# A gated-linear-attention and soft-mixture kernel, rewritten from pairs of heads over whole sequences to units of 128 tokens with all heads

## The chip, the cores and the metric

The kernel runs on one NeuronCore of a Trainium2 chip. The metric is device time in microseconds (us) of one execution. PE is TensorE (matmuls; PEld are its weight loads), DVE is VectorE, ACT is ScalarE, POOL is GpSimd, and SP is the queue that issues all DMA transfers. All data is float32. In the profile a float32 matmul stands as two MATMUL instructions, and a transpose as one.

## The reference

```python
# B, H, S, D = 4, 8, 768, 48; N = B * S = 3072 tokens of 384 columns; 8 experts of 4 slots, F = 1024
f = 1 / (1 + exp(-f_logit))
for t in range(S):                                    # per batch b and head h, state is D x D
    state = f[t][:, None] * state + outer(k[t], v[t])
    y[t] = q[t] @ state
x = y.transpose(0, 2, 1, 3).reshape(3072, 384)
logits = x @ phi                                      # 3072 x 32 slots
d = softmax(logits, over the tokens); c = softmax(logits, over the slots)
slot_input = d.T @ x                                  # 32 x 384
slot_out[e] = relu(slot_input[e] @ w1[e]) @ w2[e]     # 8 experts, 4 slots each
out = c @ slot_out                                    # 3072 x 384
```

## The kernel before

**Attention, one pair of heads at a time.** 32 heads (4 sequences x 8) are 16 pairs; a pair lies on 112 partitions, 64 r + d for head r and channel d, with all 768 tokens along the free axis. f, k and q of a pair come as six loads of 48 rows (`load_dqk`, L226 to L230), v as two of 64 rows (L232 to L235). DVE makes the decays of all 768 tokens: it adds 1 to exp(-f) (L252), and runs a scan (`decay_scan`, L258) that multiplies them up and starts anew every 64 tokens, which gives G; ACT takes its logarithm and the inverse (L266, L270), POOL multiplies k by G (L262) and q by P = 1 / G (L282). PE transposes k' (L290), makes 64x64 blocks of scores k' against q' (L302), which DVE masks (L305), and the products k'^T v of all 12 chunks (L321). A second scan on DVE (`state`, L334), with P at the chunks' ends spread over the columns (L275), carries the state through all chunks at once. The outputs are masked scores times v (`intra`, L348) and q' times states (`inter`, L362, whose moving operand takes every ninth or fourth column of the scan's result); ACT copies them to x (L367).

**Mixture.** As soon as a sequence is done, its x is transposed (L383), multiplied by phi (L390), exponentiated under a running maximum, and summed into the slots' inputs (L450). After the last pair the last sequence does the same in pieces (L399 to L418), then come the experts: `up` (L592), transposes of the hidden values (`turn`, L602), `down` in column parts of 232 and 152 (L629), the sum of the slots' columns (L643), and `combine` (L654), which multiplies the softmax over the slots by slot_out, in two parts of 12 bits at one pass per matmul. Copies (L657) and stores (L661) follow.

**Order.** The program is a list of (time, function) sorted by time (`at`, `run_atoms`); the times are a period T = 7.6 a pair and offsets in OFF, moved by tables (FK, CK, TK). They set only the order: `keep_order` makes each engine take its instructions as written. SP's queue is one of these engines. w1 is loaded during the attention, w2 into buffers as the attention leaves them.

## Time and profile before

| what | value |
|---|---|
| runs | 227.75, 230.16, 230.81 us; median 230.16 us |
| profiled execution | span 228.6 us, first to last instruction; the median of the runs lies 1.6 us above |
| busy share of the span | PE 86%, PEld 65%, DVE 78%, ACT 42%, POOL 29% |
| DMA | 49.35 MB, mean 216 GB/s; 28536 packets, 18512 of them under 2 KB |
| granted TensorE clock | 0.892 of full, mean over the span |

The span is the time from the first to the last instruction of one profiled execution. A row of a timeline gives start, duration, engine, source line, operation, output and input and count; a row of a group gives count, busy time and the mean of one in ns, then the engine's idle time before it and what ended that. A row of a window gives each engine's busy time (and count of instructions) in that stretch, then the granted clock, the DMA engines' busy share and the rate.

### The profile page before, as it was taken

How to read it: one execution, taken by the hardware profiler on the slowest of the kernel's cores; microseconds unless marked ns; L12 is line 12 of the kernel's file. 1: busy time of each engine (PE TensorE's matmuls, PEld its weight loads, DVE VectorE, ACT ScalarE, POOL GpSimd, SP SyncE). 2: the span in 40 equal slices, each digit the busy share in tenths (PEclk: the TensorE clock that was granted, in tenths of full speed). 3: DMA queues.
4: the chain of work that ended last, by engine and by line, in shares of the span. 5: the costliest groups of instructions: out<-in, count | busy, mean ns of one | idle time of the engine just before them, and what ended most of it. 6: DMA issues, size and time to landing. Idle time of an engine off the chain costs nothing.

```text
span 228.6 us, 6760 instructions
## 1 busy us (share of the span) xinstructions
PE 197.4 (86%) x2782; PEld 149.2 (65%) x2782; DVE 178.4 (78%) x322; ACT 96.9 (42%) x208; POOL 66.0 (29%) x62
## 2 busy tenths in 40 slices
PE   6598799889799599999959979999999899989820
PEld 6577678677678386887838567887756435547710
DVE  6999999999999899999998999999892352204640
ACT  7444346435575224567525255562323323103420
...
GB/s 169 230 131 200 201 229 178 244 241 252 246 220 185 95 135 149 258 211 231 206 202 108 278 181 159 233 0 217 335 289 342 346 204 326 378 179 125 339 316 66
DMA packets 28536, 49.35 MB, mean 216 GB/s; under 512 B 3664, under 2 KB 18512, under 8 KB 28496
## 3 DMA queue, kind: packets, MB, share of 16 engines
q1 hardware_dynamic: 28496, 48.82, 74.7%
...
HBM read 44.09 MB, written 4.72 MB: 214 GB/s over the span
## 4 chain that ended last, share of the span: by engine, by line
DVE 55%; PE 29%; DMA 7%; issue 4%; ACT 2%; DVEq 0%; ACTq 0%
DVE sb L334 18%; DVE gb L258 10%; DVE pb L275 7%; DMA w1b<-in_w_dram 7%; DVE scb L305 5%; PE py L362 4%; DVE eb L252 4%; DVE kvp L331 3%; PE py L348 3%; PE pi L450 3%; PE kvp L321 3%; PE pf L654 3%; PE ph L592 2%; PE po L629 2%; PE psc L302 2%
## 5 line engine op out<-in xcount | busy, mean ns | idle before, releaser
L334 DVE TENSOR_TENSOR_SCAN sb<-kvp,pb 48x432 f32<-48x432 f32 (+1 forms) x64 | 51.1, 798 | 1.3
L262 POOL TENSOR_TENSOR kb<-kb,gb 112x768 f32<-112x768 f32 (+1 forms) x17 | 29.7, 1749 | 64.0 <-DVE gb L258 51.2
L362 PE MATMUL py<-sb,qb 112*64 112x96 f32 x352 | 39.8, 356 | 0.0
L302 PE MATMUL psc<-qb,kb 48*64 48x64 f32 x768 | 32.3, 240 | 3.9 <-POOL vb L200 2.6
L302 PEld LDWEIGHTS psc<-qb,kb 48*64 48x64 f32 x768 | 26.3, 147 | 12.5 <-issue 6.1
L282 POOL TENSOR_TENSOR qb<-qb,eb 112x768 f32<-112x768 f32 (+1 forms) x15 | 26.7, 1778 | 23.4 <-ACT eb L270 22.6
L362 PEld LDWEIGHTS py<-sb,qb 112*64 112x64 f32 x352 | 27.5, 159 | 5.4 <-issue 2.5
L258 DVE TENSOR_TENSOR_SCAN gb<-eb,d 112x768 f32<-112x768 f32 (+1 forms) x17 | 28.3, 1664 | 1.6
L348 PE MATMUL py<-vb,scb 128*64 128x96 f32 x384 | 29.2, 272 | 0.0
L321 PE MATMUL kvp<-vb,ktb 128*48 128x96 f32 (+1 forms) x384 | 22.6, 272 | 5.5 <-DVE sb L334 3.9
L348 PEld LDWEIGHTS py<-vb,scb 128*64 128x64 f32 x384 | 24.4, 153 | 4.2 <-issue 3.2
L321 PEld LDWEIGHTS kvp<-vb,ktb 128*48 128x48 f32 x384 | 20.1, 143 | 7.8 <-DVE sb L334 5.3
L367 ACT COPY xb<-py 128x384 f32<-128x384 f32 (+1 forms) x32 | 12.7, 398 | 23.5 <-PE py L362 23.5
L248 ACT ACTIVATE eb<-fb 112x768 f32<-112x768 f32 (+1 forms) x17 | 13.6, 803 | 19.2 <-POOL qb L282 12.4
L275 DVE COPY pb<-eb 112x384 f32<-112x384 f32 (+1 forms) x32 | 20.7, 690 | 0.5
L266 ACT ACTIVATE eb<-gb 112x768 f32<-112x768 f32 (+1 forms) x17 | 13.7, 809 | 10.4 <-DVE gb L258 10.4
L290 PE MATMUL pk<-ident,kb 112*128 112x112 f32 x96 | 17.8, 304 | 0.0
L291 ACT COPY ktb<-pk 128x336 f32<-128x336 f32 x32 | 13.8, 437 | 7.4 <-PE pk L290 7.3
L305 DVE TENSOR_TENSOR scb<-psc,mask 128x384 f32<-128x384 f32 x32 | 16.4, 551 | 0.3
L270 ACT ACTIVATE eb<-eb 112x768 f32<-112x768 f32 (+1 forms) x17 | 13.7, 808 | 0.3
L290 PEld LDWEIGHTS pk<-ident,kb 112*128 112x128 f32 x96 | 10.9, 157 | 3.2 <-issue 0.7
L252 DVE TENSOR_SCALAR eb<-eb 112x768 f32<-112x768 f32 (+1 forms) x17 | 10.3, 606 | 1.2 <-ACT eb L248 1.2
(181 smaller groups left out, 277.6 us busy)
## 6 DMA issues: line engine op xcount, KB each, us to landing
...
```

The lines of the kernel that those rows point to most:

```text
L252: nc.vector.tensor_scalar(e, e, 1.0, G_LIM, op0=ALU.add, op1=ALU.min)
L258: nc.vector.tensor_tensor_scan(part(own(gb, i), h), e, d, 1.0, op0=ALU.mult, op1=ALU.min)
L262: (nc.gpsimd if ENG["dk"] == 2 or i < 2 else nc.vector).tensor_tensor(t, t, part(use(gb, i), h), op=ALU.mult)
L275: eng("pend")(t[:PW, :, : c1 - c0], e[:, c0:c1].unsqueeze(1).broadcast_to([PW, D, c1 - c0]))
L282: (nc.gpsimd if i > 1 and ENG["dq"] == 2 or (i, h) == (1, 1) else nc.vector).tensor_tensor(t, t, part(use(eb[i % NEB], i), h), op=ALU.mult)
L290: nc.tensor.transpose(pk[:, mm], kq[:PW, 128 * m : 128 * m + 128], ident[:PW, :PW])
L302: nc.tensor.matmul(scp[i, r][64 * j : 64 * j + 64, 64 * m : 64 * m + 64], kq[rs, cs], qq[rs, cs], start=True, stop=True)
L305: nc.vector.tensor_tensor(own(scb[i % NSC], i)[:, r], scp[i, r][:, : NM * C].rearrange("q (m t) -> q m t", t=C), mask.unsqueeze(1).broadca ...
L321: nc.tensor.matmul(pk[64 * r : 64 * r + D, cs], kr[:, m, 64 * r : 64 * r + D], vv[:, :nj, m, r], start=True, stop=True)
L334: nc.vector.tensor_tensor_scan(st[h][rs, r].rearrange("p e c -> p (e c)"), kvh[rs, : D * n], pe[rs].rearrange("p e c -> p (e c)"), 0.0, op ...
L348: nc.tensor.matmul(py[64 * w : 64 * w + 64, M - Ms[0], :, r], sc[:, r, m], vv[:, :, m, r], start=M == Ms[0] and r == 0, stop=False, skip_g ...
L362: nc.tensor.matmul(py[64 * w : 64 * w + 64, M - Ms[0], j], qt[:PW, C * c : C * c + C], sc, start=False, stop=(M, j) == (Ms[-1], 1), skip_g ...
```

## The change

The whole program is another. It has 12 units of 128 tokens instead of 16 pairs of 768 tokens: unit u holds tokens 128 (u // 2) to 128 (u // 2) + 127 of the two sequences 2 (u % 2) and 2 (u % 2) + 1, with all 8 heads of both: 16 heads, as 8 pairs `a` on partitions 64 r + d. The gate sums are made by PE: softplus(-f) of a unit (one exp and one ln on ACT, tokens on partitions) is multiplied by a triangle of ones (`d_cum`, 8 matmuls of 128x128x128), and ACT makes G and P from the result (`d_g`, `d_p`). Chunks are still 64 tokens (j = 0, 1), with the decay running over both; the state is carried by three adds and products of 384 columns on DVE (`state_1`, `state_t`, `state_2`) in place of the scans. `kv`, `inter`, `scores` and `intra` are 32 matmuls each of one head and one chunk (`inter` in two halves of 16, one before `scores`, one after `intra`), placed so that consecutive ones lie in the four quarters of the array (rows 0 or 64, columns 0 or 64) and the two row halves write different PSUM banks. PSUM is four tiles of two banks: PA for gate sums and the mixture, PB for outputs, PC for the transposes of k', then kv, then the transposes of x, PD for scores. Every load has 128 rows: k and q come padded to 64 channels, 4 KB a row, w1 and w2 as 16 pieces each of 128 rows of 6 KB. The mixture works on groups of two units (256 tokens of two sequences). w2 and the output are split in two column halves, one load a piece; `combine` is a float32 product of 32 rows for each of four 32-row groups. The warm-up matmuls that stood at the start are no longer called. The order is again a sorted list, with T = 6.9.

```diff
...
-NCH = S // C  # chunks of a sequence
-NM = NCH // 2  # pairs of chunks
-NG = NM // 2  # blocks of 256 tokens
+L = 128
+NU = 12
+NV = 6
...
+T = 6.9
+OFF = dict(
+    lf=6.2 - 4 * T, lk=4.4 - 3 * T, lq=6.6 - 3 * T, lv=6.5 - 2 * T,
+    exp=4.25 - 2 * T, ln=5.3 - 2 * T, cum=0.9 - T, g=1.95 - T, p=3.1 - T, dk=3.1 - T, dq=5.55 - T, pend=8.0 - T,
+    kt=0, ktok=0.95, kv=2.1, s1=2.8, p2=3.5, sc=3.75, st=3.4, mask=4.5, intra=5.9, p1=6.2,
+    y=T + 0.1, s2=T + 1.1, xt=T + 4.45, xe=T + 5.75,
+    lg=2 * T + 5.2, mx=2 * T + 5.7, et=2 * T + 6.3, tr=3 * T + 5.2, el=3 * T + 5.7, pin=4 * T + 5.2, join=4 * T + 5.7,
+)
...
+    PA, PB, PC, PD = (pp.tile([128, 2, 512], F32, tag=n, name=n) for n in ("pa", "pb", "pc", "pd"))
...
-    def load_dqk(bufs, src, i, h=None):
-        t = own(bufs[i % len(bufs)], i)
-        cs = slice(0, S) if h is None else slice(HALF * h, HALF * h + HALF)
-        for r in (1, 0):
-            nc.sync.dma_start(t[64 * r : 64 * r + D, cs], src[i, r, :, cs])
+    def load(name, src, u):
+        nc.sync.dma_start(R(name, u), src[u])
...
-    def decay_exp(i, h=None):
-        nc.scalar.activation(part(own(eb[i % NEB], i), h), part(use(fb[i % NF], i), h), AF.Exp, scale=-1.0)
-    def decay_e(i, h=None):
-        e = part(use(eb[i % NEB], i), h)
-        nc.vector.tensor_scalar(e, e, 1.0, G_LIM, op0=ALU.add, op1=ALU.min)
-    def decay_scan(i, h=None):
-        e, d = part(use(eb[i % NEB], i), h), part(flat(d1), h)
-        # the product, never less than its last factor, starts anew with each chunk
-        nc.vector.tensor_copy(chunks(d)[:, :, 0], chunks(e)[:, :, 0])
-        nc.vector.tensor_tensor_scan(part(own(gb, i), h), e, d, 1.0, op0=ALU.mult, op1=ALU.min)
-    def decay_k(i, h=None):
-        t = part(use(kb[i % NK], i), h)
-        (nc.gpsimd if ENG["dk"] == 2 or i < 2 else nc.vector).tensor_tensor(t, t, part(use(gb, i), h), op=ALU.mult)
-    def decay_ln(i, h=None):
-        e, g = part(use(eb[i % NEB], i), h), part(use(gb, i), h)
-        nc.scalar.activation(e, g, AF.Ln)
-    def decay_inv(i, h=None):
-        e = part(use(eb[i % NEB], i), h)
-        nc.scalar.activation(e, e, AF.Exp, scale=-1.0)
+    def d_exp(u):
+        nc.scalar.activation(R("f", u), R("f", u), AF.Exp, scale=-1.0, accum_out=esum[:, u : u + 1])
+    def d_ln(u):
+        nc.scalar.activation(
+            R("sp").rearrange("p (a d) -> p a d", d=64)[:, :, :D], R("f", u).rearrange("p (a d) -> p a d", d=D), AF.Ln, bias=1.0,
+        )
+    def d_cum(u):
+        sp = R("sp").rearrange("p (a x) -> p a x", x=128)
+        for a in range(8):
+            nc.tensor.matmul(PA[:, a // 4, 128 * (a % 4) : 128 * (a % 4) + 128], sp[:, a], tri, start=True, stop=True)
+    def d_g(u):
+        nc.scalar.activation(R("g"), PA.rearrange("p b x -> p (b x)"), AF.Exp)
+    def d_p(u):
+        nc.scalar.activation(R("p"), PA.rearrange("p b x -> p (b x)"), AF.Exp, scale=-1.0)
+    def d_k(u):
+        nc.gpsimd.tensor_tensor(R("k", u), R("k", u), R("g"), op=ALU.mult)
+    def d_q(u):
+        nc.gpsimd.tensor_tensor(R("q", u), R("q", u), R("p"), op=ALU.mult)
...
-    def score(i, r, m):
-        kq, qq = use(kb[i % NK], i), use(qb[i % NQ], i)
-        if m == 0:
-            scp[i, r] = PS([128, 512], f"sc{r}", "psc", 1)
-        rs = slice(64 * r, 64 * r + D)
-        for j in range(2):
-            cs = slice(C * (2 * m + j), C * (2 * m + j) + C)
-            nc.tensor.matmul(scp[i, r][64 * j : 64 * j + 64, 64 * m : 64 * m + 64], kq[rs, cs], qq[rs, cs], start=True, stop=True)
+    def kt(u):
+        kq = heads(R("k", u), L)
+        for a in range(8):
+            nc.tensor.transpose(PC[:, a // 4, 128 * (a % 4) : 128 * (a % 4) + 128], kq[:, a], ident)
+    def kt_copy(u):
+        nc.scalar.copy(heads(R("kt"), D), PC.rearrange("p b (a d) -> p (b a) d", d=64)[:, :, :D])
+    def scores(u):
+        kq, qq = heads(R("k", u), L), heads(R("q", u), L)
+        for a in range(8):
+            for r in range(2):
+                rs = slice(64 * r, 64 * r + D)
+                for j in range(2):
+                    js = slice(64 * j, 64 * j + 64)
+                    nc.tensor.matmul(PD[js, r, 64 * a : 64 * a + 64], kq[rs, a, js], qq[rs, a, js], start=True, stop=True)
+    def s_mask(u):
+        nc.vector.tensor_tensor(
+            heads(R("sc"), C), PD.rearrange("p r (a t) -> p (r a) t", t=C), mask.unsqueeze(1).broadcast_to([128, 16, C]), op=ALU.mult,
+        )
...
-        for r in range(2):
-            rs = slice(64 * r, 64 * r + D)
-            nc.vector.tensor_tensor_scan(
-                st[h][rs, r].rearrange("p e c -> p (e c)"), kvh[rs, : D * n], pe[rs].rearrange("p e c -> p (e c)"), 0.0, op0=ALU.add, op1=ALU.mult,
-            )
+    def kv(u):
+        kr, vv = R("kt").rearrange("p (a r d) -> p a r d", r=2, d=D), R("v", u).rearrange("p (a r d) -> p a r d", r=2, d=D)
+        for a in range(8):
+            for r in range(2):
+                for j in range(1 if u // 2 == NV - 1 else 2):
+                    js = slice(64 * j, 64 * j + 64)
+                    nc.tensor.matmul(PC[64 * r : 64 * r + D, j, D * a : D * a + D], kr[js, a, r], vv[js, a, r], start=True, stop=True)
+    def state_1(u):
+        nc.vector.tensor_tensor(S1(u), PC[:, 0, :DM], S0(u), op=ALU.add)
+    def state_t(u):
+        if u + 2 < NU:
+            nc.vector.tensor_tensor(R("t"), PC[:, 1, :DM], S1(u), op=ALU.add)
+    def state_2(u):
+        if u + 2 < NU:
+            nc.vector.tensor_tensor(heads(S0(u + 2), D), heads(R("t"), D), pend[:, u].unsqueeze(2).broadcast_to([128, 8, D]), op=ALU.mult)
+    def inter(u, ph):
+        qq = heads(R("q", u), L)
+        for p in range(4):
+            for r in range(2):
+                j = r if ph else 1 - r
+                st, rs = heads((S0, S1)[j](u), D), slice(64 * r, 64 * r + D)
+                for w in range(2):
+                    nc.tensor.matmul(
+                        PB[64 * w : 64 * w + 64, j, 96 * p + D * r : 96 * p + D * r + D], qq[rs, 4 * w + p, 64 * j : 64 * j + 64],
+                        st[rs, 4 * w + p], start=not ph and p == 0, stop=ph == 1 and p == 3, skip_group_check=True,
+                    )
+    def intra(u):
+        sc, vv = R("sc").rearrange("p (r a t) -> p r a t", r=2, t=C), R("v", u).rearrange("p (a r d) -> p a r d", r=2, d=D)
+        for p in range(4):
+            for r in range(2):
+                for j in range(2):
+                    js = slice(64 * j, 64 * j + 64)
+                    for w in range(2):
+                        nc.tensor.matmul(
+                            PB[64 * w : 64 * w + 64, j, 96 * p + D * r : 96 * p + D * r + D], sc[js, r, 4 * w + p], vv[js, 4 * w + p, r],
+                            start=False, stop=False, skip_group_check=True,
+                        )
+    def y_copy(u):
+        nc.vector.tensor_copy(xs[u], PB[:, :, :DM])
+    def x_tr(u):
+        for j in range(2):
+            for c in range(3):
+                nc.tensor.transpose(PC[:, j, 128 * c : 128 * c + 128], xs[u][:, j, 128 * c : 128 * c + 128], ident)
+    def x_copy(u, fast=False):
+        n = 2 * (u % 2)
+        t = xT[:, n : n + 2].rearrange("p n c t -> p n (c t)")
...
+        else:
+            nc.vector.tensor_copy(t, PC[:, :, :DM])
...
+    def c_pin(g):
+        for n in range(4):
+            nc.tensor.matmul(PA[32 * n : 32 * n + 32, 1, :DM], el[:, g, 0, 32 * n : 32 * n + 32], xs[2 * g + n // 2][:, n % 2], start=True, stop=True)
+    def c_join(g):
+        if g:
+            nc.vector.scalar_tensor_tensor(pin, pin, alpha, PA[:, 1, :DM], op0=ALU.mult, op1=ALU.add)
...
+    W1 = [(2 * qq + j, hf) for j in range(2) for hf in range(2) for qq in range(4)]
+    W2 = [(h, 2 * qq + j) for h in range(NH) for j in range(2) for qq in range(4)]
+    def load_w1(i):
+        e, hf = W1[i]
+        w1u[e, hf] = wr[:, i].rearrange("p (c x) -> p c x", c=3)
+        nc.sync.dma_start(wr[:, i], w1[e, hf])
+    def load_w2(i, home):
+        h, e = W2[i]
+        w2u[h, e] = home.rearrange("p (k d) -> p k d", k=8)
+        nc.sync.dma_start(home, w2[h, e])
...
+    def down(h, j, kk):
+        for qq in range(4):
+            nc.tensor.matmul(
+                PD[32 * qq : 32 * qq + 32, h, :HC], hT[:, j, kk, 32 * qq : 32 * qq + 32], w2u[h, 2 * qq + j][:, kk],
+                start=j == 0 and kk == 0, stop=j == 1 and kk == 7,
+            )
...
+    FIN = [(PA, PC), (PB, PA), (PC, PB)]
+    def combine(h, y):
+        hs_ = slice(HC * h, HC * h + HC)
+        for x in range(2):
+            for n in range(4):
+                ns = slice(32 * n, 32 * n + 32)
+                nc.tensor.matmul(FIN[y][n // 2][:, n % 2, HC * x : HC * x + HC], ct[ns, 2 * y + x], s4[ns, hs_], start=True, stop=True)
+        for z in range(2):
+            dst = stage[h][:, 2 * y : 2 * y + 2, 2 * z : 2 * z + 2].rearrange("p v n d -> p n v d")
+            (nc.vector.tensor_copy if z else nc.scalar.copy)(dst, FIN[y][z][:, :, : 2 * HC].rearrange("p n (v d) -> p n v d", v=2))
+    def store(h, y):
+        nc.sync.dma_start(out[h][:, 8 * y : 8 * y + 8], stage[h][:, 2 * y : 2 * y + 2].rearrange("p v n d -> p (v n) d"))
...
+    for i in range(16):
+        at((i - 1) * T - 6.5 if i < 13 else (i - 13) * 0.1 + 11 * T - 7, load_w1, i)
+    zl = 11 * T
+    homes = [(zl - 6.0, x) for x in span("f")] + [(zl + 1.5, x) for x in span("sp", 2)] + [(zl + 4.6, x) for x in span("k", 2)]
+    homes += [(zl + 6.65, x) for x in span("kt", 2)] + [(zl + 6.65, x) for x in span("q", 2)]
...
-    a = {}
-    for n, name in (("q", "q"), ("k", "k"), ("f", "f_logit")):
-        a[n] = inputs[name].reshape(NP, 2, S, D).transpose(0, 1, 3, 2)
-    x = inputs["v"].reshape(NP, 2, NM, 2, C, D)  # pair, r, m, j, s, e
-    a["v"] = x.transpose(0, 3, 4, 2, 1, 5).reshape(NP, 2, C, NM * 2 * D)
-    a["vt"] = inputs["v"].reshape(NP, 2, S, D).transpose(0, 1, 3, 2)
+_OUTS = [((NH, 128, 4 * NV, HC), "float32")]
+    for n, name in (("q", "q"), ("k", "k")):
+        x = inputs[name].reshape(2, 2, 4, 2, NV, L, D).transpose(4, 0, 3, 6, 1, 2, 5)
+        y = np.zeros((NV, 2, 2, 64, 2, 4, L), np.float32)
+        y[:, :, :, :D] = x
+        a[n] = y.reshape(NU, 128, 1024)
+    for n, name in (("f", "f_logit"), ("v", "v")):
+        a[n] = inputs[name].reshape(2, 2, H, NV, L, D).transpose(3, 0, 4, 1, 2, 5).reshape(NU, 128, 768)
```

**PE, a pair and a unit of the steady middle.** Names: pk is the transposes of k', psc the scores, py the outputs, kvp the products k'^T v, pxt the transposes of x. Before, one pair:

```order
L302 MATMUL psc<-qb_74,kb_70 64x64 x12
L290 MATMUL pk<-ident,kb_70 128x112 x3
L302 MATMUL psc<-qb_74,kb_70 64x64 x10
L383 MATMUL pxt<-ident,xb_86 128x128 x3
L348 MATMUL py<-vb_80,scb_77 64x2x48 x8
L321 MATMUL kvp_115<-vb_78,ktb_84 48x2x48 x8
L321 MATMUL kvp_116<-vb_78,ktb_84 48x2x48 x2
L321 MATMUL kvp_116<-vb_78,ktb_84 48x48 x2
L383 MATMUL pxt<-ident,xb_86 128x128 x3
L362 MATMUL py<-sb_82,qb_73 64x96 x7
L348 MATMUL py<-vb_80,scb_77 64x2x48 x4
```

Now, unit 5 (arena holds all of the attention's SBUF data; L216 is `kt`, L192 `d_cum` of the next unit, L243 `kv`, L270 `inter`, L228 `scores`, L298 the transposes of x of the unit before, L342 and L312 the mixture, L282 `intra`):

```order
L216 MATMUL pc<-ident,arena 128x128 x8
L192 MATMUL pa<-tri,arena 128x128 x8
L243 MATMUL pc<-arena 48x48 x32
L270 MATMUL pb<-arena 64x48 x16
L228 MATMUL pd<-arena 64x64 x32
L298 MATMUL pc<-ident,arena 128x128 x6
L342 MATMUL pa<-arena,el 32x384 x4
L312 MATMUL pa<-arena,phs 32x128 x12
L282 MATMUL pb<-arena 64x48 x32
L270 MATMUL pb<-arena 64x48 x16
```

Before, pieces of neighbouring pairs stand between each other; now one unit's steps stand in the order of their dependence, and only `d_cum` of the next unit, the transposes of x of the unit before and the mixture stand between them.

**DVE, the same places.** Before, one pair (gb is G, sb the states, pb the spread P):

```order
L305 TENSOR_TENSOR scb_77<-psc,mask 128x384 x2
L252 TENSOR_SCALAR eb_68<-eb_68 112x768
L257 COPY d_89<-eb_68 112x12
L258 SCALAR_TENSOR_TENSOR gb<-eb_68,d_89 112x768
L334 SCALAR_TENSOR_TENSOR sb_82<-kvp_115,pb 48x432 x2
L331 TENSOR_TENSOR kvp_116<-kvp_116,sb_82 48x48 x2
L334 SCALAR_TENSOR_TENSOR sb_82<-kvp_116,pb 48x192 x2
L275 COPY pb<-eb_67 112x48x8
L275 COPY pb<-eb_67 112x48x3
```

Now, unit 5 (L252 `state_1`, L256 `state_t`, L231 the mask, L349 to L324 the mixture's join and maximum, L307 the copy of the transposed x, L290 the copy of the outputs, L260 `state_2`):

```order
L252 TENSOR_TENSOR arena<-pc,arena 128x384
L256 TENSOR_TENSOR arena<-pc,arena 128x384
L231 TENSOR_TENSOR arena<-pd,mask 128x1024
L349 COPY pin<-pa 128x384
L322 TENSOR_REDUCE small<-pa 128x1
L324 TENSOR_TENSOR nmx<-nmx,small 128x1
L307 COPY arena<-pc 128x768
L290 COPY arena<-pb 128x768
L260 TENSOR_TENSOR arena<-arena,check 128x384
```

The scans, the spread of P and the adding of 1 are gone from DVE; the copies of the outputs and of the transposed x, which ACT made, have come to it, and the copy that frees PC (L307) stands behind the mixture's instructions.

More of the change, by code (lines that the diff above doesn't have):

```diff
@@ L144, in gla_soft_moe_kernel @@
[L144 to L157 removed]
+    size, place = 0, {}
@@ L159, in gla_soft_moe_kernel, with R @@
+    region("xT", 1, 1536)
+    arena = P([128, size], "arena")
+    def R(name, i=0):
+        o, n, w = place[name]
+        i %= n
+        return arena[:, o + i * w : o + i * w + w]
+    wr = P([128, 16, UN], "wr")
+    el = P([128, NV, 2, 128], "el")
+    lt = P([128, 128], "lt")
+    et = P([128, 128], "et")
+    ct = P([128, NV, 128], "ct")
+    pin = P([128, DM], "pin")
     nmx = P([128, 2], "nmx")
     sms = P([128, 2], "sms")
-    nmb = P([128, 4], "nmb")
+    small = P([128, 12], "small")
@@ L211, in warm @@
-    def warm(count):
-        pw = PS([128, 128], "y", "pw") if count else None
-        for n in range(count):
-            nc.tensor.matmul(pw, ones, ones, start=True, stop=True)
-    def consts_3():
+        for j in range(2):
+            js = slice(64 * j, 64 * j + 64)
+            nc.gpsimd.affine_select(mask[js], ones[js, :C], pattern=[[1, C]], compare_op=ALU.is_ge, fill=0.0, base=0, channel_multiplier=-1)
+        nc.vector.memset(PC, 0.0)
+        nc.vector.memset(R("s", 0), 0.0)
+        nc.vector.memset(R("s", 2), 0.0)
@@ L219, in consts_3, with warm @@
+        nc.vector.memset(PB, 0.0)
+    def warm(n):
+        for _ in range(n):
+            nc.tensor.matmul(PD[:, 1, :128], ones, ones, start=True, stop=True)
+    def consts_1():
         for g in range(4):
@@ new lines, in gla_soft_moe_kernel, with t_max2, t_psi @@
+    gm, wb, zs, rzs = small[:, 2:3], small[:, 3:4], small[:, 4:5], small[:, 5:6]
+    def t_max2():
+        nc.tensor.matmul(PD[:, 0, :1], gr.rearrange("q g s -> q (g s)"), ones[:1, :1], start=True, stop=True)
+        nc.vector.tensor_copy(gm, PD[:, 0, :1])
+        nc.scalar.activation(wb, nmL, AF.Exp, bias=gm, scale=-1.0)
+        nc.vector.tensor_scalar(wd, same[:, :NS], wb, None, op0=ALU.mult)
+    def t_psi():
+        psi = PD[:, 1, :96].rearrange("p (c s) -> p c s", c=3)
+        for c in range(3):
+            for g in range(4):
+                nc.tensor.matmul(psi[32 * g : 32 * g + 32, c], pin[:, 128 * c + 32 * g : 128 * c + 32 * g + 32], wd, start=True, stop=True)
+        nc.vector.tensor_copy(si, psi)
@@ new lines, in c_soft2, with c_ct @@
+    def c_soft2():
+        cb = cmv.unsqueeze(3).broadcast_to([128, NV, 4, NS])
+        nc.vector.tensor_reduce(cmv, ls, axis=AX.X, op=ALU.add)
+        nc.vector.tensor_scalar(cm, cm, 1e-9, None, op0=ALU.add)
+        nc.vector.reciprocal(cm, cm)
+        nc.vector.tensor_tensor(ls, ls, cb, op=ALU.mult)
+    def c_ct(h):
+        for x in range(3):
+            nc.tensor.transpose(PC[:, h, 128 * x : 128 * x + 128], el[:, 3 * h + x, 1], ident)
+        nc.scalar.copy(ct[:, 3 * h : 3 * h + 3], PC[:, h, :384].rearrange("p (v t) -> p v t", v=3))
@@ new lines, in gla_soft_moe_kernel @@
+    o = OFF
+    at(-100, consts_0)
+    for u in range(NU):
+        z = u * T
+        for key, name, src in (("lf", "f", f), ("lk", "k", k), ("lq", "q", q), ("lv", "v", v)):
+            at(z + o[key], load, name, src, u)
+        at(z + o["exp"], d_exp, u)
+        at(z + o["ln"], d_ln, u)
+        at(z + o["cum"], d_cum, u)
+        at(z + o["g"], d_g, u)
+        at(z + o["p"], d_p, u)
+        at(z + o["dk"], d_k, u)
+        at(z + o["dq"], d_q, u)
+        at(z + o["pend"], d_pend, u)
+        at(z + o["kt"], kt, u)
+        at(z + o["ktok"], kt_copy, u)
+        at(z + o["kv"], kv, u)
+        at(z + o["sc"], scores, u)
+        at(z + o["s1"], state_1, u)
+        at(z + o["p2"], inter, u, 0)
+        at(z + o["p1"], inter, u, 1)
+        at(z + o["mask"], s_mask, u)
+        at(z + o["intra"], intra, u)
+        at(z + o["st"], state_t, u)
+        at(z + o["y"], y_copy, u)
+        at(z + o["s2"], state_2, u)
+        if u < NU - 1:
+            at(z + o["xt"], x_tr, u)
+            at(z + o["xe"], x_copy, u)
```

868 lines of the change are left out of this document (233 added, 635 removed).

## The prediction

> **What bounds the kernel now.** I read the chain that ended last first, then the span cut into its stages.
>
> ```profile
> DVE 55%; PE 29%; DMA 7%; issue 4%; ACT 2%; DVEq 0%; ACTq 0%
> DVE sb L334 18%; DVE gb L258 10%; DVE pb L275 7%; DMA w1b<-in_w_dram 7%; DVE scb L305 5%; PE py L362 4%; DVE eb L252 4%; DVE kvp L331 3%; PE py L348 3%; PE pi L450 3%; PE kvp L321 3%; PE pf L654 3%; PE ph L592 2%; PE po L629 2%; PE psc L302 2%
> ```
>
> ```profile
> core 0: us, PE busy (x) PEld busy (x) DVE busy (x) ACT busy (x) POOL busy (x), PEclk, DMA share, GB/s
> 0.00:14.00 14.00, 8.80 (x72) 8.18 (x76) 11.68 (x20) 8.25 (x13) 9.27 (x20) 0.92 0.84 190
> 14.00:165.00 151.00, 137.33 (x2070) 110.06 (x2066) 141.80 (x240) 72.97 (x157) 56.13 (x34) 0.87 0.73 197
> 183.00:205.00 22.00, 21.33 (x269) 10.68 (x269) 5.86 (x17) 4.08 (x8) 0.00 (x0) 1.00 0.80 279
> 205.00:219.00 14.00, 12.45 (x178) 9.95 (x170) 8.28 (x17) 5.99 (x14) 0.00 (x0) 1.00 0.72 234
> 190.00:200.00 10.00, 10.00 (x135) 5.72 (x129) 2.47 (x6) 1.67 (x3) 0.00 (x0) 1.00 1.00 350
> 40.00:60.00 20.00, 16.14 (x277) 13.18 (x275) 19.12 (x37) 8.94 (x18) 9.00 (x6) 0.99 1.04 243
> 117.51:120.93 3.42, 1.12 (x13) 0.75 (x13) 2.78 (x7) 0.84 (x3) 0.00 (x0) 1.00 0.50 135
> 120.93:124.34 3.41, 3.41 (x49) 3.29 (x50) 2.98 (x8) 2.08 (x7) 1.95 (x1) 0.50 0.43 133
> ```
>
> Up to 165 the chain is VectorE: the scans (L334, L258), the spread of P (L275), the mask. DVE is busy for 141.8 of 151.0 us there. The attention ends at 175.05 (below), the rest is the tail. In the chain two waits stand for weights:
>
> ```profile
> 189.03 6.37 DMA w1b<-in_w_dram
> 195.42 8.63 DMA w1b<-in_w_dram
> 218.23 0.48 DVE w1b L657
> ```
>
> So a pair costs some 9.1 us of attention (16 pairs, with DVE as its measure), and the tail 53.5 us, of which the last 9.9 lie behind the last copy (218.71 to 228.6).
>
> **The change, part by part.** It removes all scans, the spread and the adding of 1 from DVE (some 6.5 of those 9.1 us), so DVE ceases to be the bound: it keeps the mask, three state steps and two copies. What takes its place is a chain across engines, and since PE takes its steps as written, one unit can't start before the last one is through. The PE prices come from these rows:
>
> ```profile
> 2.21 6.28 PE L215 MATMUL pw<-ones 128*128 128x128 f32 x28 [2.21 <-POOL ones L177]
> 64.78 0.33 PE L302 MATMUL psc<-qb,kb 48*64 48x64 f32 x4
> 65.52 0.80 PE L302 MATMUL psc<-qb,kb 48*64 48x64 f32 x24
> 66.69 0.80 PE L302 MATMUL psc<-qb,kb 48*64 48x64 f32 x20
> 66.25 0.51 PE L290 MATMUL pk<-ident,kb 112*128 112x112 f32 x3
> 182.40 0.40 PE L572 MATMUL psi<-wd,pin 128*32 128x32 f32 x24
> 182.50 0.29 PE L572 MATMUL psi<-wd,pin 128*32 128x32 f32 x13
> 183.20 5.36 PE L592 MATMUL ph<-w1b,el 128*32 128x512 f32 x48
> ```
>
> 28 instructions of 128 columns took 6.28 us at half clock, .224 each, so .112 at full clock; a transpose is one of these. 20 against 4 small instructions differ by .47 us, .0294 each, and these ran in two column halves: .0588 for a round that fills both. The group of 24 in the same .80 us holds four of the other row half, which cost nothing: so I price a round of four quarters at .0588 too. 32-column rounds cost .04 (11 instructions more, .11 us more). kv has 48 columns: between .04 and .0588, I take .045. The 64 instructions of `scores` or `intra` are 16 rounds, .94 us, an `inter` half .47, `kv` .72. The other engines:
>
> ```profile
> L367 ACT COPY xb<-py 128x384 f32<-128x384 f32 x16 | 7.6, 477 | 13.8 <-PE py L362 13.8
> L367 ACT COPY xb<-py 128x192 f32<-128x192 f32 x16 | 5.1, 318 | 9.7 <-PE py L362 9.7
> L603 DVE TENSOR_TENSOR w1b<-pht,pb 128x512 f32<-128x512 f32 x4 | 2.7, 689 | 10.3 <-PE pht L602 10.3
> L305 DVE TENSOR_TENSOR scb<-psc,mask 128x384 f32<-128x384 f32 x32 | 16.4, 551 | 0.3
> L262 POOL TENSOR_TENSOR kb<-kb,gb 112x768 f32<-112x768 f32 x15 | 27.5, 1834 | 61.7 <-DVE gb L258 48.9 <-PE pk L290 4.8 <-DMA kb<-in_k_dram 3.8
> L262 POOL TENSOR_TENSOR kb<-kb,gb 112x384 f32<-112x384 f32 x2 | 2.2, 1114 | 2.3 <-DVE gb L258 2.3
> L479 DVE SCALAR_TENSOR_TENSOR pin<-pi,nmb,pin 128x384 f32<-128x384 f32 x2 | 1.2, 618 | 0.1
> L428 DVE TENSOR_REDUCE nmb<-lt 128x1 f32<-128x192 f32 x2 | 0.7, 353 | 0.1
> ```
>
> By the two sizes of each, an ACT copy out of PSUM costs .83 ns a column more (768 columns .80 us, 1024 columns 1.01), DVE 1.08 (mask of 1024: 1.24; copy of 768: .97; state step of 384: .55), POOL 1.88 (1024: 2.31).
>
> One unit, from its first transpose at full clock: `kt` 8 x .112 to .93; the next unit's `d_cum`, 16 x .112, to 2.70, beside which ACT's copy (.80) is hidden; `kv` to 3.57, seen by DVE at 3.75 (a hand-over between engines taken as .1 to .2); `state_1` to 4.35; `inter` and `scores` 1.41, seen at 5.95; mask to 7.2; `intra` and second `inter` 1.41, to 8.7; with the hand-over **8.9 us**. `state_t` and the transposes of x (.67) stand beside the mask and cost nothing while the mask takes 1.24; without it they would add .7. Behind the mask DVE's copy L307 (.97) frees PC by 8.3, before 8.7. In units 5, 7 and 9, L349 (.62), a second small step (.22), L322 (.35) and L324 (.15) are queued before L307, so the next `kt` waits for it: **10.0**. Off this path, per unit: ACT 4.6 us (exp, ln, two of 1024, a copy), POOL 2 x 2.31, DVE about 5, and DMA 2.62 MB (f and v .39 each, k and q .52, one weight piece .79), which at the 350 GB/s of 190 to 200 takes 7.5. All are hidden with 1.4 us to spare for the DMA, which is the thinnest cover.
>
> Start: f lands and exp, ln, sums (at half clock 16 x .224 = 3.6), G and k' follow each other; before's first scores began at 11.0, after half a pair's f; I take 14.0 for the first `kt`. Unit 0 has no warm clock: its 6.2 us of PE on the path, with about two thirds of it at half clock, make 13. Then seven units of 8.9 (62.3), three of 10 (30), the last with half a `kv` 8.4: the attention ends at **127.7**, before at 175.05:
>
> ```profile
> 174.69 0.36 PE L362 MATMUL py<-sb,qb 112*64 112x96 f32 x2
> ```
>
> Tail: from there to `up` 8.4 (before 183.20 - 175.05 = 8.15, the same chain of transposes, maximum, exponentials and sums). `up` has 96 instructions at .112, 10.7, and a transpose with mask behind it, 12.3. A column half of `down` is 32 rounds of 192 columns; by L592 (48 instructions, 12 rounds of 512, 5.36: .447 a round) .168 each, 5.4, with turn and transposes between 6.9 and, in the second half with the first `combine` parts (12 rounds, 2.0) and its waits, 8.3. Then slot sums, three combines and their copies 6.2 and the last stores and end 9.9, as before. Sum 52.0, against 53.5: the waits for weights go. Eleven w2 pieces can't start before the attention's buffers come free; 8.65 MB at 350 GB/s are 25 us, so they land some 28 us behind the attention, and the last are needed at 31. If that cover of 2.5 us is lost, each us more comes straight on the end.
>
> 127.7 + 52.0 = 179.7 of span, against 228.6; the median of the runs stood 1.6 above the profiled span: **181 us**.
>
> Bounds of the prices that no row shows: a round of four quarters lies between .0294 (all four for the price of one) and .1176 (four times that, nothing beside another). Four stages of 16, 8, 16 and 8 such rounds and `kv`'s make 64 a unit, so -1.8 or +3.5 us per unit on the path (-21, +42); I take .0588, as the row with both row halves says. A hand-over between .05 and .35 (there are four on the path) moves 12 units by -4 or +10. The start lies between 11 and 17.
>
> **Rivals.** (1) *A price for each instruction.* Every small instruction costs .0294, whatever quarter it goes to: 181 + 42 = **223**, about -3%. For it: only four of the group of 24 used the other row half. Against it: they cost nothing, and 11 more of L572 took .11 us, .010 each. The Trainium skill, page "TensorE: Matmul & The Clock Gate", section "Wait — 56ns, not 53.3ns?", gives a milder form: two matmuls never start less than about 25 ns apart, however small. By that page the 256 instructions of a unit take 6.4 us instead of 3.5, an estimate of 35 more and 216 in all; the trace disagrees with it by the .010 above, though these share one row group. Chance .09. (2) *The clock.* Granted clock was .87 in the attention, and it fell to .5 behind stretches of 3.4 us in which PE was busy for only 1.12 (rows 117.51 and 120.93). Before, 13% of clock was lost, so half clock for 26% of the time. A unit has PE busy about 7 of 8.9 us, in the worst 3.4 us (3.6 to 7.0 of the walk, with the waits for `state_1` and the mask) some 2.1. With the same 26%, 12 x 6.2 x .26 = 19 more: **200**, chance .15. That stretch holds .67 of transposes; if these didn't count, 1.4 would be left, near the 1.12 that fell. The Trainium skill, page "TensorE: Matmul & The Clock Gate", "Part 4: PE-mode transpose", says just that, that transposes don't count as PE work for the clock; no row of before tells it apart. (3) *The other side: half clock throughout.* The chain has its own pauses; at half clock PE takes 6.2 more a unit on the path while the pauses stay, so each stretch could fall short again and the clock would never come back. 11 x 6.2 = 68: **249**; it turns slower from 49 us, 72% of the units. Against it: at half clock PE is busier, and the row at 120.93 shows 3.41 of 3.41 busy, which brought the clock back. Chance .05. (4) *DMA at 243 GB/s*, the rate of 40 to 60 with queues full at 1.04: 51.9 MB in all (k and q padded 12.6, f and v 9.4, weights 25.2, output 4.7) take 214, with the end 224. It needs 4 KB rows to run no better than the short ones, against the 350 above with 6 KB rows.
>
> ```profile
> DMA packets 28536, 49.35 MB, mean 216 GB/s; under 512 B 3664, under 2 KB 18512, under 8 KB 28496
> ```
>
> 18512 of 28536 packets were under 2 KB before; now none of a load is under 3 KB. Chance .04.
>
> **How the numbers follow.** Forecast (165 to 195) .64; clock at 195 to 210 .15; a price for each instruction .09; half clock throughout .05; DMA .04; below 164 .03. The range 164 to 206 takes the forecast and most of the second case, and leaves out the others; the bounds' far ends (160 and 223) lie outside it. Within 2% (about what a measurement of this kernel can tell from no change) gets .03, from the ends of rivals 1 and 4. Slower .06, rival 3 with a small part of those; faster .91.
>
> **What would show it.** Right: groups of 64 small instructions in .9 to 1.0 us; a unit every 8.9 us and three at 10; clock near 1.0 from some 20 us on; DVE below 60% in the attention; rates of 280 GB/s there without PE waiting for a load; the attention ended near 128 and a tail of 52. Wrong: such a group in 1.6 or more (rival 1), windows of .5 clock among the units (2, 3), PE waiting for `k` or `f` loads (4), or a wait for w2 in `down`.

## The result and the profile after

The changed kernel takes 215.35 us (median of four runs, 210.89 to 221.82); the kernel before took 229.22 beside it. The ratio is 0.926, with a 95% interval of 0.916 to 0.935: faster by some 7%, where 181 us and 21% were forecast. (The ratio compares the runs near each kernel's fastest.) The changed kernel spreads over 5%, the one before over 1.3%. The profiled execution took 210.89 us, its span is 209.2.

The chain that ended last names only the last 8 us here, so the stages carry the reading. Windows of the changed kernel: the attention from its first transposes of k' to its last `inter`, then five pieces of the tail (up to `up`; `up` with its turns; both `down` parts; the last sums and copies; what lies behind the last copy), then a pause of PE and the 3.4 us behind it.

```profile
core 0: us, PE busy (x) PEld busy (x) DVE busy (x) ACT busy (x) POOL busy (x), PEclk, DMA share, GB/s
13.12:147.12 134.00, 107.68 (x3506) 95.80 (x3506) 57.85 (x90) 50.89 (x81) 55.98 (x44) 0.96 0.75 263
147.12:158.14 11.02, 6.66 (x79) 3.23 (x78) 5.63 (x17) 2.15 (x10) 0.00 (x0) 0.85 0.64 244
158.14:173.53 15.39, 14.77 (x111) 4.55 (x111) 5.83 (x11) 2.98 (x5) 0.00 (x0) 0.89 0.64 253
173.53:191.67 18.14, 16.50 (x317) 10.66 (x317) 5.00 (x7) 3.82 (x7) 0.00 (x0) 1.00 0.41 167
191.67:198.00 6.33, 3.69 (x50) 2.51 (x50) 2.88 (x4) 2.71 (x4) 0.00 (x0) 1.00 0.78 314
198.00:209.20 11.20, 0.27 (x1) 0.08 (x1) 1.02 (x6) 0.00 (x0) 0.00 (x0) 0.55 0.34 132
74.30:76.20 1.90, 0.24 (x15) 0.10 (x4) 0.00 (x0) 0.97 (x3) 1.90 (x2) 1.00 0.31 127
76.30:79.70 3.40, 3.40 (x42) 2.38 (x46) 1.22 (x1) 0.00 (x0) 1.27 (x2) 0.50 0.39 105
```

DVE has indeed ceased to be the bound: 57.85 of 134.0 us. But nothing else has become one by its busy time: PE 107.68, POOL 55.98, DMA share 0.75. And from 74.3 to 76.2 PE stands still, though nothing that another engine does there is what PE needs next; behind it the clock falls to 0.5. The waits of PE between 13 and 147 us (in total, times, longest):

```profile
PE pb L270 <- DVE arena L252: 10.0, 12, 0.8
PE pc L298 <- issue: 4.0, 3, 1.7
PE pc L216 <- POOL arena L201: 3.6, 1, 3.6
PE pd L228 <- issue: 3.4, 3, 1.7
PE pb L282 <- DVE arena L231: 3.1, 5, 1.4
PE pc L243 <- issue: 1.9, 2, 1.3
PE pc L216 <- DVE arena L307: 1.3, 2, 0.7
PE pb L282 <- issue: 1.0, 2, 0.6
```

The waits for L252, L231 and L307 are those of my walk, and the one for POOL is the start of the first unit. The rows with `issue` are not in it: PE stops in the middle of `scores`, of `kv`, of three transposes of x, for up to 1.7 us, and waits for nothing that the profile shows. One of them, in the timeline (start, duration):

```profile
98.69 0.55 PE L298 MATMUL pc<-ident,arena 128*128 128x128 f32 x3
100.94 0.55 PE L298 MATMUL pc<-ident,arena 128*128 128x128 f32 x3 [1.70 <-issue]
```

I counted PE's own instructions in the trace (each matmul pair is a weight load and a MATMUL, and some waits stand between) and wrote beside the counts when the 16 KB transfers of the queue named "instruction" ran, which are blocks of the program, 256 instructions of 64 bytes. Every pause over 0.4 us without a visible cause lies at 193 plus a multiple of 256. Four of the 27 block ends of the attention, from the trace (a stall is counted from the start of the last weight load before it):

```
instruction  PE came there  transfer of next block  PE went on   stall
       3009          71.55       68.12 to  69.00        71.55     none
       3265          74.27       74.02 to  74.97        76.23     1.97
       4545          98.86       98.69 to  99.65       100.94     2.08
       4801         104.20      102.81 to 103.75       105.21     1.02
```

At the 11 stalls over 0.4 us PE goes on 1.2 to 1.5 us after the transfer's end. Over all of the attention the transfer starts 0.75 to 3.8 us after the block before was entered (1.9 in the mean) and takes 1.0. The three parts together: here **PE can't enter a block earlier than 3.1 to 6.2 us, in the mean 4.3, after the last**. The 11 stalls make 14.0 us. In the kernel before a pair of heads took 9.1 us and not much more than one block.

### The profile page after: what moved, and what is told of

Read it like the earlier page. It is cut to its first block, busy times and chain, and to the rows that moved or that the text cites. A ratio compares the mean times of both kernels' runs of the same rounds, so it can differ in the third digit from the quotient of the medians.

```text
span 209.2 us, 8817 instructions
## 1 busy us (share of the span) xinstructions
PE 153.3 (73%) x4076; PEld 120.3 (58%) x4076; DVE 81.7 (39%) x137; ACT 69.1 (33%) x113; POOL 59.9 (29%) x55
## 5 line engine op out<-in xcount | busy, mean ns | idle before, releaser
L201 POOL TENSOR_TENSOR arena<-arena 128x1024 f32<-128x1024 f32 x12 | 28.4, 2365 | 73.4 <-ACT arena L195 73.4
L192 PE MATMUL pa<-tri,arena 128*128 128x128 f32 x192 | 27.2, 303 | 5.8 <-ACT arena L185 5.8
L192 PEld LDWEIGHTS pa<-tri,arena 128*128 128x128 f32 x192 | 26.1, 219 | 5.7 <-issue 5.7
L204 POOL TENSOR_TENSOR arena<-arena 128x1024 f32<-128x1024 f32 x12 | 28.3, 2358 | 0.0
L270 PE MATMUL pb<-arena 48*64 48x48 f32 x768 | 17.0, 223 | 10.7 <-DVE arena L252 10.0
L252 DVE TENSOR_TENSOR arena<-pc,arena 128x384 f32<-128x384 f32 x12 | 6.7, 558 | 43.8 <-PE pc L243 29.5
L231 DVE TENSOR_TENSOR arena<-pd,mask 128x1024 f32<-128x1024 f32 x12 | 14.7, 1224 | 21.3 <-PE pd L228 21.3
L270 PEld LDWEIGHTS pb<-arena 48*64 48x64 f32 x768 | 14.7, 137 | 12.0 <-issue 12.0
L216 PE MATMUL pc<-ident,arena 128*128 128x128 f32 x96 | 14.8, 303 | 4.9 <-POOL arena L201 3.6
L228 PE MATMUL pd<-arena 48*64 48x64 f32 x768 | 15.7, 227 | 3.4 <-issue 3.4
L195 ACT ACTIVATE arena<-pa 128x1024 f32<-128x1024 f32 x12 | 12.3, 1024 | 17.3 <-PE pa L192 17.3
L282 PE MATMUL pb<-arena 64*64 64x48 f32 x768 | 14.7, 221 | 4.1 <-DVE arena L231 3.1
L282 PEld LDWEIGHTS pb<-arena 64*64 64x64 f32 x768 | 12.8, 135 | 6.8 <-DVE arena L231 4.3
L228 PEld LDWEIGHTS pd<-arena 48*64 48x64 f32 x768 | 14.0, 141 | 3.8 <-issue 3.8
L298 PE MATMUL pc<-ident,arena 128*128 128x128 f32 x72 | 12.4, 307 | 4.6 <-issue 4.0
L216 PEld LDWEIGHTS pc<-ident,arena 128*128 128x128 f32 x96 | 11.7, 155 | 6.0 <-POOL arena L201 3.9
L290 DVE COPY arena<-pb 128x768 f32<-128x768 f32 x12 | 11.5, 955 | 7.2 <-PE pb L270 7.1
L243 PE MATMUL pc<-arena 64*48 64x48 f32 x704 | 11.7, 208 | 2.8 <-issue 1.9
L243 PEld LDWEIGHTS pc<-arena 64*48 64x48 f32 x704 | 10.0, 122 | 4.6 <-issue 2.2
L198 ACT ACTIVATE arena<-pa 128x1024 f32<-128x1024 f32 x12 | 12.2, 1018 | 0.0
```

The costliest lines, as they stand in the source:

```text
L192: nc.tensor.matmul(PA[:, a // 4, 128 * (a % 4) : 128 * (a % 4) + 128], sp[:, a], tri, start=True, stop=True)
L195: nc.scalar.activation(R("g"), PA.rearrange("p b x -> p (b x)"), AF.Exp)
L198: nc.scalar.activation(R("p"), PA.rearrange("p b x -> p (b x)"), AF.Exp, scale=-1.0)
L201: nc.gpsimd.tensor_tensor(R("k", u), R("k", u), R("g"), op=ALU.mult)
L204: nc.gpsimd.tensor_tensor(R("q", u), R("q", u), R("p"), op=ALU.mult)
L216: nc.tensor.transpose(PC[:, a // 4, 128 * (a % 4) : 128 * (a % 4) + 128], kq[:, a], ident)
```

## The experiments

**Half the instructions for the same columns (e1).** In `scores`, for example:

```diff
-        for a in range(8):
+        for a in range(0, 8, 2):
...
-                    nc.tensor.matmul(PD[js, r, 64 * a : 64 * a + 64], kq[rs, a, js], qq[rs, a, js], start=True, stop=True)
+                    nc.tensor.matmul(
+                        PD[js, r, 64 * a : 64 * a + 128].rearrange("p (b t) -> p b t", t=64), kq[rs, a, js], qq[rs, a : a + 2, js], start=True, stop=True,
+                    )
```

> Each matmul of kv, scores, inter and intra now takes the moving columns of two head pairs at once (96 or 128 columns instead of 48 or 64), so there are half as many of these instructions for the same columns; every second pair of heads gets its product with the other pair's weights, so the output is not the reference's. Theory A (PE waits for its own program, which comes in blocks of 256 instructions; the changed kernel's stalls stand exactly at every 256th): about 20 blocks instead of 32, the stalls at block ends (14.6 us before 151 us) fall below 3 us, two of the half-clock stretches go with them, span 188 to 194 against 209.2. Theory B (the stalls belong to the array, the semaphores or PSUM and not to the program's length): as many stalls, span 205 to 212.

Measured: 188.91 us (ratio 0.824, 0.818 to 0.831), span 187.1, a little under theory A's range. PE's waits from 13 to 125 us have no row with `issue` left:

```profile
PE pb L275 <- DVE arena L257: 10.0, 12, 0.8
PE pb L288 <- DVE arena L233: 3.7, 7, 1.4
PE pc L216 <- POOL arena L201: 3.6, 1, 3.6
PE pc L216 <- DVE arena L314: 3.2, 3, 1.1
```

At block ends one stall of 0.43 is left. From unit 1 on, units now follow each other at 8.45 to 9.0 us, 10.3 to 10.5 with the mixture. A group of half as many instructions takes nearly the same time, so the array's work is nearly the same; `scores` of a unit here and in the changed kernel:

```profile
28.44 1.08 PE L228 MATMUL pd<-arena 48*64 48x128 f32 x32
```

```profile
110.52 1.16 PE L228 MATMUL pd<-arena 48*64 48x64 f32 x64
```

The five groups of a unit together became 0.65 us shorter (`inter` 0.68 to 0.56 and 0.65 to 0.51, `kv` 0.94 to 0.88, `intra` 1.15 to 0.89, `scores` 0.08); of the 22.1 us by which the attention became shorter (134.0 to 111.9), the stalls are some 14 and these groups some 8. This account is rough: PE's waits for DVE grew by 2.5 us and the half clock got shorter.

**The dose (e10, e11).** e10 has the halves only in `scores` and `intra`; e11 issues `scores` twice.

```diff
         at(z + o["sc"], scores, u)
+        at(z + o["sc"], scores, u)
```

> As e1, but only scores and intra have half the instructions (every second pair of heads is multiplied by the other pair's weights there; kv and inter are whole): 239 instruction pairs a unit in place of 303, 26 blocks of program. Theory A: between the changed kernel (14.0 us of stalls at block ends) and e1 (none in the units): 3 to 7 us, span 194 to 201. Theory B (the stalls came from kv's or inter's products, and not from the length): as many stalls as before or none.

> The changed kernel with scores issued twice (the second time writes the same values): 64 more instruction pairs a unit, 6 more blocks of program, and .95 us more of PE's own time per unit, 11.4 in all. Theory A: besides the 11.4 the stalls at block ends grow from 14 to 22 to 30 us, span 228 to 238. Theory B: the stalls stay at 12 to 16 us, span 217 to 224.

Stalls over 0.4 us at block ends, inside the attention, from the traces:

```
kernel        pairs a unit  stalls  us in all  attention   span
e1                     175       1        0.4      111.9  187.1
e10                    239       7        5.7      121.2  196.1
changed                303      11       14.0      134.0  209.2
e11                    367      12       21.1      168.3  242.4
```

The stalls grow with the instructions through the whole row, as theory A says, and B's numbers came nowhere. A's own numbers held but for e11: its stalls are just under the forecast 22 to 30 us, and its span is over 238. Besides 7.1 us of stalls and 11.4 of PE's own time, the clock stood at 0.5 for 47.8 us of its attention, against 10.2 in the changed kernel. Its waits with `issue` (13 to 182 us) are nearly all in the doubled step:

```profile
PE pd L228 <- issue: 14.1, 9, 2.5
PE pc L298 <- issue: 2.0, 1, 2.0
PE pb L282 <- issue: 1.4, 1, 1.4
```

**A dose that measured something else (e3).**

```diff
+    def extra(u):
+        for x in range(64):
+            nc.tensor.matmul(PB[:32, 0, 400:401], ident[:32, :32], ident[:32, :1], start=False, stop=False, skip_group_check=True)
...
+        at(z + o["intra"], extra, u)
         at(z + o["intra"], intra, u)
```

> 64 matmuls of 32x32 by one column per unit are added ahead of intra, into PSUM columns that nobody reads. Theory A: half a block of program more per unit; a block took 4.2 us in the mean from one to the next, so 1.5 to 2.1 us more per unit, span 227 to 234. Theory B: at .01 to .0147 us each they take .6 to .9 us, partly beside the mask, span 209 to 216.

Measured: 283.69 us, outside both. I had miscounted (64 matmuls are 128 pairs, a whole block), and the group is slow by itself, probably since all lie in one place of the array (this wasn't tested apart):

```profile
77.88 4.21 PE L291 MATMUL pb<-ident 32*32 32x1 f32 x128
```

That is .033 us each, 4.2 to 5.9 us a unit (9.0 and 7.0 in the first two), and the clock was at half for 88 of 209 us of attention, though PE's rows show it busy. It says nothing for or against blocks of program; e11 was made in its place.

**What the blocks wait behind (e2, e7).** e2 loads 64 KB of each w1 piece instead of 768:

```diff
-        w1u[e, hf] = wr[:, i].rearrange("p (c x) -> p c x", c=3)
-        nc.sync.dma_start(wr[:, i], w1[e, hf])
+        w1u[e, hf] = wr[:, i, :128].unsqueeze(1).broadcast_to([128, 4, 128])
+        nc.sync.dma_start(wr[:, i, :128], w1[e, hf][:, :128])
...
```

> The w1 pieces are cut from 768 KB to 64 KB (each row's first 128 columns, read four times over by up; the output is not the reference's). 11.5 MB fewer bytes, same instructions on every engine. Theory A1 (the blocks of program wait behind data in the DMA engines): the delay from a block's start to the next block's transfer falls from 1.9 us in the mean to about 1, the stalls of the attention from 14.6 to 3 to 6 us, span 194 to 200. Theory A2 (a block takes its 4 us whatever else is moved): stalls 12 to 16 us, span 206 to 211.

Measured: 203.03 us (ratio 0.885, 0.877 to 0.893), span of the profiled execution 204.3; stalls 7.0 us, mean delay 1.5. It lies between A1 and A2 and in the range of neither: without 11.5 MB half of the stalls go. At the six that stay, the delay was still 0.7 to 2.3 us, so they aren't explained by w1's bytes; what the transfer waits for there is open. e7 moves the same bytes in other bursts:

```diff
...
-        at((i - 1) * T - 6.5 if i < 13 else (i - 13) * 0.1 + 11 * T - 7, load_w1, i)
+        if i < 13:
+            at((i - 1) * T - 2.45, load_w1, i, 0)
+            at((i - 1) * T - 0.25, load_w1, i, 1)
...
```

> Each w1 piece of the attention is loaded as two halves of 3 KB rows, one behind k's load and one behind q's, in place of one load of 768 KB behind q and v. Same bytes, same PE program. If the next block of program waits behind whole bursts of data (A1): bursts of 1.3 MB twice a unit in place of 0.9 and 1.7, the mean delay from a block's start to the next block's transfer falls from 1.9 to 1.4 to 1.6 us, stalls from 14 to 8 to 11 us, span 202 to 208 against 209.2. If it waits for the share of the DMA engines' time alone: no change, 207 to 217 as the changed kernel's own runs.

Measured: 218.65 us (ratio 0.955, 0.946 to 0.963), mean delay 2.1, stalls 19.6 us. No gain from smaller bursts is to be seen, against both forecasts. Whether they did harm isn't shown: the changed kernel's own runs reach 221.82, and e9 below, with the same halves, had 16.2 us of stalls.

**Fewer instructions in earnest (e4).** Products over all 128 tokens in place of halves:

```diff
...
-                for j in range(2):
-                    js = slice(64 * j, 64 * j + 64)
-                    nc.tensor.matmul(PD[js, r, 64 * a : 64 * a + 64], kq[rs, a, js], qq[rs, a, js], start=True, stop=True)
+                nc.tensor.matmul(PD[:, r, 128 * p : 128 * p + 128], kq[rs, 4 * h + p], qq[rs, 4 * h + p], start=True, stop=True)
...
```

> The changed kernel with no halves of 64 tokens: scores are 16 products of 128x128 a unit in two groups of 8, masked in two steps of 1024 columns; kv, inter and intra are 16 matmuls each over all 128 tokens; the second state step is gone; the steps of a unit are ordered anew so that PE never waits for the mask or the state (gate sums first). 175 instruction pairs a unit in place of 303: 1.4 blocks of program. By my prices PE is then busy for some 9.4 us of a unit and waits for nothing. Theory A (blocks of program, 4.3 us each): they hide beside it, no stall over 1 us at a block's end, a unit every 9.3 to 9.8 us, the attention ends near 125 and the span is 186 to 192, though PE has more columns to stream than in the changed kernel. Theory B (array and chain alone set a unit): PE busy 9.4 a unit is more than the 9.1 of the changed kernel's shortest unit, so the span is 207 to 215.

Measured: 300.13 us, far outside both. Two of my own errors are in it. The next loads of v and q stand ahead of the last reads of the old ones, so part of the products take other tokens, and PE waits 24.1 us for v. And a unit's PE work is some 12.6 us, not 9.4; two of its rows at full clock:

```profile
98.01 1.10 PE L253 MATMUL pb<-arena 48*128 48x48 f32 x16
100.85 1.99 PE L262 MATMUL pb<-arena 128*128 128x48 f32 x16
```

With weights of 128 rows and 128 columns (L262) an instruction takes .112 us though only 48 columns move (16 in 1.99 less some .2 of the last one's length), as much as with 128 moving. With 48 rows, in two row halves (L253), it takes half of that; the 48-column products of the changed kernel, in four quarters, .0147 (`kv`, 64 in .94). So the narrow tiles that need so many instructions are also the quick ones here. Stalls over .4 at block ends there were none in its units, but it doesn't settle A against B, since PE waited elsewhere and a block lasted 11 us or more.

**The tail (e5, e6, e8, e9).** e5 and e6 stand on e4, and only their tails are read.

```diff
...
-        (c_lg, NV - 1), (c_max, NV - 1), (c_join, NV - 2), (c_exp, NV - 1), (t_max,), (c_tr, NV - 1), (c_copy, NV - 1), (t_max2,), (c_pin, NV - 1), (c_join, NV - 1),
+        (c_lg, NV - 1), (warm, 2), (c_max, NV - 1), (c_join, NV - 2), (c_exp, NV - 1), (t_max,), (warm, 4),
+        (c_tr, NV - 1), (c_copy, NV - 1), (t_max2,), (warm, 1), (c_pin, NV - 1), (warm, 3), (c_join, NV - 1),
...
```

> e4 with 11 matmuls of 128x128x128 into PSUM columns that nobody reads, in the pauses that PE has between the last sequence's logits and up. In the changed kernel the clock fell to .5 for 6.8 us there (154.8 to 161.6), and the first of up's four parts took 4.49 us in place of 2.78. Theory C (the pauses cost the clock): no half clock behind the logits, 2 to 4 us less than e4. Rival: the added matmuls stand in PE's way and cost what they bring, within 1 us of e4.

> e5 with the seven small steps of the range flag (DVE and one transpose, 198.0 to 199.5 in the changed kernel, behind the last copy) moved to places behind the sums and beside up, where DVE waits. The branch that reads the flag stays at the end. If the end is the flag and then the branch in a row: 1.3 to 1.6 us less than e5. If the end is set by the stores' landing (the last one starts at the last copy): within .3 us of e5.

As wholes, 295.04 and 296.94 us, they can't be told from e4. In the tails: the first part of `up` in the changed kernel, in e4 and in e5,

```profile
158.14 4.49 PE L400 MATMUL pc<-wr,lt 128*32 128x512 f32 x24 [0.38 <-DVE lt L393]
```

```profile
244.22 3.89 PE L380 MATMUL pc<-wr,lt 128*32 128x512 f32 x24 [0.38 <-DVE lt L373]
```

```profile
240.20 2.78 PE L380 MATMUL pc<-wr,lt 128*32 128x512 f32 x24
```

so the pauses did cost the clock, 1.1 us here where theory C said 2 to 4 (1.7 in the changed kernel, 4.49 against 2.78), and the added matmuls nothing: from the last `inter` to `up` it took 10.86 in e4 and 10.83 in e5. From the last `combine` matmul to the end e4 took 12.7, e5 12.8, e6 9.9, more of a gain than the forecast 1.3 to 1.6; but in e6 `down` then waited .86 for the flag's PSUM bank. e8 puts all of this into the changed kernel, the flag in another bank, and the second transposes of the softmax behind the slot sums.

> The changed kernel with three edits of the tail: 11 warm matmuls between the last logits and up, the flag's steps moved ahead (its transpose behind the last turn, in PSUM bank PA), and the second transposes of the softmax put behind the first slot sums. From the last inter to the end the changed kernel took 62.1 us. Theory C (half clock 1.1 to 1.8 us, flag 1.6 to 2.9, wait for the slot sums .4): 56.5 to 59 us there; the whole 206 to 213, since the stalls of the attention stay as they are. Rival (each of the three is hidden by a wait that takes its place): 61 to 62.5.

> e7 and e8 together: the two act in different stretches, so the gains add: 198 to 205 if both theories hold, 206 to 213 if only the tail's does.

e8 took 213.73 us, 207.45 to 216.34, too wide a spread for a ratio; e9 211.33, ratio 0.923 (0.916 to 0.931), as the changed kernel. The tail of e8 is 57.06 us against 62.1 (58.7 in e9), within theory C's 56.5 to 59:

```profile
155.34:165.61 10.27, 8.84 (x100) 5.75 (x99) 5.60 (x17) 2.15 (x10) 0.00 (x0) 1.00 0.73 283
165.61:179.29 13.68, 13.07 (x112) 4.27 (x111) 6.21 (x14) 2.98 (x5) 0.00 (x0) 1.00 0.72 286
179.29:196.93 17.64, 16.47 (x319) 10.81 (x318) 5.46 (x10) 3.82 (x7) 0.00 (x0) 1.00 0.43 173
196.93:204.23 7.30, 4.99 (x50) 3.39 (x50) 2.87 (x3) 2.71 (x4) 0.00 (x0) 0.71 0.76 310
204.23:212.40 8.17, 0.00 (x0) 0.00 (x0) 0.00 (x0) 0.00 (x0) 0.00 (x0) 0.50 0.39 145
```

The end behind the last copy is 8.17 in place of 11.20, `up` with its turns 13.68 in place of 15.39; the last sums and copies took 7.30 in place of 6.33, with a clock of 0.71. But the attentions of e8 and e9 took 142.6 and 138.8 us (stalls 14.7 and 16.2, half clock 33.6 and 23.2), more than the 134.0 of the changed kernel's own profile, and that hid the five. Why the clock was lower there is open. So e9 is no better than the changed kernel by more than its spread.

## Why the prediction was wrong

The sign was right, the size was not: the gain was a third of the forecast. The sum was 179.7 of span; it was 209.2, 29.5 more: start and first unit -1.0, units 1 to 11 +20.4 (121.1 for 100.7), tail +10.1.

- **The step that failed is the walk of one unit**, "One unit, from its first transpose at full clock". Its prices were nearly right. A unit without a stall, in the trace:

```profile
105.46 1.09 PE L216 MATMUL pc<-ident,arena 128*128 128x128 f32 x8
106.39 1.95 PE L192 MATMUL pa<-tri,arena 128*128 128x128 f32 x16
108.27 0.94 PE L243 MATMUL pc<-arena 64*48 64x48 f32 x64
109.34 0.56 DVE L252 TENSOR_TENSOR arena<-pc,arena 128x384 f32<-128x384 f32 x1 [2.35 <-PE pc L243]
111.73 1.23 DVE L231 TENSOR_TENSOR arena<-pd,mask 128x1024 f32<-128x1024 f32 x1 [1.24 <-PE pd L228]
113.01 1.15 PE L282 MATMUL pb<-arena 64*64 64x48 f32 x64 [0.31 <-DVE arena L231]
114.56 0.33 PE L216 MATMUL pc<-ident,arena 128*128 128x128 f32 x1
```

 It took 9.10 us from one `kt` to the next, where I had 8.9; the next unit, with the mixture and no stall over .4, took 10.75 where I had 10.0. What the walk lacked is a resource: PE's own program. A unit has 303 pairs, 2.4 blocks, and at 4.3 us each they need 10.2 us, more than the 8.9 of the chain. Of the 20.4 us, 13.1 are stalls at block ends in units 1 to 11, and half clock followed two of them (the one of 1.97 up to 76.23, from 76.3; the one of 1.47 up to 138.81, from 141.2); that the stalls set it off is likely but not tested apart. The chain's own excess and the slower stretches share the other 7, which I didn't separate further.
- The view that would have made me ask was on the page of before, among its DMA queues (packets, MB, share of the span); the page of the changed kernel has the second line:

```profile
q8 instruction: 24, 0.39, 0.7%
```

```profile
q8 instruction: 34, 0.56, 1.0%
```

 Before, these are 24 blocks in 228.6 us, 9.5 us each; in its trace no two start less than 6.0 us apart until the branch at the end. The changed kernel's 4076 pairs are 32 blocks, 2782 were 22 (two more come at the end in both), and 27 of the 32 fell into an attention that I forecast at 114 us: 4.2 us each. The Trainium skill, page "Runtime: NRT & Kernel Launch", section "Instruction fetch mechanics", says that PE's program comes in blocks of 16 KiB, 256 instructions, and that a crossing is mostly hidden. The size agrees with this trace; that it is hidden does not, with 14.0 us of 134.
- **Rivals.** Price for each instruction: its total, 223, was nearer than my forecast, but the mechanism is refuted, since the groups took .94 to 1.16 us for 64 (with some .2 for the last one's length), as forecast, and e1 halved the instructions without halving their time. What an instruction did cost was its way to PE, 4.3 us for 256. Half clock: real, but small: 10.2 us of the attention in the profiled execution; the granted clock was 0.96 there, so the 26% of that rival were not reached. (The clock's record begins at 18.3 us; before that, the first unit's eight transposes took 1.97 us in place of 1.09, as the prediction's cold first unit had it.) In the profiled executions of e7 to e9 it came to 23 to 34 us, so this rival had more in it than one trace shows. Half clock throughout and DMA at 243 GB/s did not occur (263 GB/s, and none of PE's long waits is for k or f). One reading against half clock throughout was wrong: the busy row at 120.93 didn't bring the clock back by itself, the next 3.4 us were at half clock too, and it came back at 127.8.
- **That DMA is hidden "with 1.4 us to spare"** held for data: PE waited for no load in the attention. But those transfers delayed the program's, which I had not counted among them; in e2, without most of w1's bytes, 7 of the 14 us were gone.
- **The tail** was taken at 52.0 and was 62.1. Blocks have little part in it: one stall of about 1 us stands in its first piece (up to 150.47), and in e1, whose tail has none, it took 61.8. The terms, forecast and measured: to `up` 8.4 and 11.0; `up` with turns 12.3 and 15.4; both `down` parts 15.2 and 18.1; last sums and copies 6.2 and 6.3; behind the last copy 9.9 and 11.2. The first was copied from before, whose chain is another, and half clock and that stall are in it too (10.27 in e8, at full clock); the second missed the half clock behind PE's pauses, 1.7 us (e5, e8), and 1.4 stay open. In `down` I had no price for the wait on the slot sums (.54 and .41; PE waited for no w2 piece), and the other 2 us are open. Behind the last copy, the flag's steps can be moved away, which gained 3.0 us (e6, e8); but they stood there before too, for 1.73 us against 1.49 now, so they don't explain the 1.3 more, which came between the flag and the end (8.1 us before, 9.7 now) and stays open.
- **What would show the prediction wrong**, as I had listed it, named windows of .5 clock among the units, which came (25.1, 76.3 and 141.2), but not a wait for the program. Of the signs that it is right, groups of 64 in .9 to 1.0 came about true (.94 to 1.16), DVE below 60% too (43%); the unit's time, the clock, the 280 GB/s, the end of the attention and the tail did not follow.
